# A planned order of attention and ReGLU feed-forward work, planned anew with other transfer times, one load hold moved, and the last copies split over two PSUM banks

## The chip, the cores and the metric

The kernel runs on one core of one Trainium2 chip. The metric is the device time of one execution in microseconds (us). A profiled execution also gives a span, from its first to its last instruction, which is about 2 us shorter than the device time.

## The reference, cut to what matters

There are 8 batches, 8 heads, 576 queries and 64 channels per head; 16 beacon keys and values stand in front of the 576 ordinary ones, so that each query sees up to 592 keys. The attention output of all batches (4608 tokens of 512 channels) goes through a feed-forward block with a ReLU gate. Inputs and output are float32.

```python
k_all = concatenate([beacon_k, k], axis=2); v_all = concatenate([beacon_v, v], axis=2)
scores = matmul(q, k_all.T) / sqrt(D);  scores = where(causal, -1e9, scores)
a = exp(scores - scores.max(-1)); a /= a.sum(-1) + 1e-09
x = (a @ v_all).transpose(0, 2, 1, 3).reshape(B * S, H * D)
out = (maximum(x @ w_gate, 0) * (x @ w_val)) @ w_out        # 512 -> 1536 -> 512
```

## The kernel before

**Work.** A batch is loaded through 8 staging tiles (`st`, 128x512 float32): K and Q by head pairs and "rests" (L545 to L628), V in 5 blocks (L631). Every staged tile is cast to bfloat16 (`rounded`, L511; V at L464 or L462), on POOL for all batches but the first, where DVE may do it as well (`ENG`). Q and K are then turned on TensorE (L522) and copied out of PSUM. Scores are computed in 64x64 tiles of the array (L740), one block of 64 queries against the keys that it may see. For each piece DVE adds the mask and takes the minimum (L688), ACT takes exp with the row sum (L695), DVE the reciprocal (L701), and POOL multiplies it in (L706). In the first batch TensorE turns the probabilities (L816); in the later ones a transposing DMA on SP's queue does (L826), one for each of four head pairs. The product with V (L836, in 128x64 tiles, and L859 for the last 16 queries) gives the token columns `xT`.

The feed-forward block takes the tokens in ten spans: 240, 336, seven times 512, and 448. I number them 0 to 9. A span is 12 times a gate (L897, relu on ACT at L908) and a value (L902, product on DVE at L913), four matmuls each, and then an output product (L928) of 12 matmuls for each 128 tokens, whose result is copied (L460 on ACT, L462 on DVE) and stored (L942). Spans 0 and 1 need the first batch alone; span 2 also needs the second.

**Weights.** They come by nine DMAs that POOL issues (L474): gate and value columns 0 to 511, 512 to 1023 and 1024 to 1535, then three row blocks of `w_out`. POOL runs in order, so each stands between other POOL work.

**The order.** No loop sets the order: every piece of work is a task with engines, a cost in us, dependences and a priority, and `Plan.order` (L183) lists them with a model of time: it takes the task that can begin first and, among those, the one of the lowest priority. A task that moves data also occupies a single "wire" for `move` us and ends a fixed time after that; a transfer may be begun at most `backlog` us before the wire is free (L203). Engines and queues then run in exactly the listed order, with semaphores. Costs and the constants at the head of the file (L20 to L57) so decide the order, and nothing else on the chip. `RANK1` is the priority of the second batch's loads.

Where the plan foresees an idle TensorE before its 160th us it lists fillers (L241 to L248): matmuls at L987 whose result nobody reads.

**Holds.** `HELD` (L38) ties three staging tiles of the second batch to weights: a one-element memset on POOL (L532) is planned after the named weight DMA has been issued, writes into the staging tile, and the tile's load waits for that write. Tile 0 is the K rest, tiles 2 and 4 are the K loads of its first two head pairs; SP's queue runs in order, so the loads behind them wait too.

**The end.** The last 64 tokens' output product is made in two halves of 256 columns, in two column tiles (partitions 0 to 63 and 64 to 127) of one bank. DVE copies one half, ACT the other, and SP and ACT each issue a store.

Of the kernel before, what the change touches and what calls it, by code (L numbers as in the profile page):

```python
# [16 lines left out]
BIG = 1e9  # L17


BACKLOG = 4.0  # L20
RANK1 = -19.0
AHEAD = 2.0
WWORK = -15.0
FILLED = 160.0
# [4 lines left out]
SWITCH = 0.1  # L29
# [5 lines left out]
PEQ = lambda b, g: b < 1  # L35
ENG = [("POOL", "DVE"), ("POOL",), ("POOL",)]
F_MOST = 3
HELD = {(1, 0): ("v", 0, 0), (1, 2): ("g", 0, 1024), (1, 4): ("v", 0, 1024)}  # L38
BEHIND = {(2, 7): (1, 1)}
MARK = 0.08  # L40
AB_FIRST = 0
# [8 lines left out]
W0 = 9.0  # L50
W_STEP = 3.4
W_ISSUE = 0.85
N_ST = 8
N_OSB = 3
FIRST_SPANS = [240, 336]
# [111 lines left out]
class Plan:  # L167
# [15 lines left out]
    def order(self):  # L183
        free = {}
        queue = {}
        for t in self.tasks:
            for e in t.engines:
                free.setdefault(e, 0.0)
                queue.setdefault(e, [])
        for t in self.tasks:  # L190
            if t.left == 0:
                for e in t.engines:
                    queue[e].append(t)
        wire = 0.0
        part = 0
        free["DMA"] = 0.8
        done = []

        def begin(t, e):
            at = t.ready  # L200
            if e == "DMA" or t.move:
                at = max(at, wire - self.backlog)
            for h in t.holds:  # L203
                if h.tile is None:
                    if h.prev is not None:
                        continue
                    if h.next is not None:
                        first = h.slots.first_pairs(sum(x.next is not None for x in t.holds))
                        if first is None:
                            return None  # L210
                        at = max(at, first)
                        continue
                    first = h.slots.first(sum(x.tile is None and x.slots is h.slots for x in t.holds) - 1)
                    if first is None:
                        return None
                    at = max(at, first)
            return max(at, free[e]), at

        while True:
            best = None  # L220
            for e in queue:
                for t in queue[e]:
                    times = begin(t, e)
                    if times is None:
                        continue
                    at, could = times
                    late = 0
                    if e == "PE":
                        late = -1 if part and t.part == part else 1 if part != t.part and at < t.ready + t.lazy else 0
                    key = (at, late, t.prio)  # L230
                    if best is None or key < best[0]:
                        best = (key, t, e)
            if best is None:
                break
            (at, _, _), t, e = best
            for x in t.engines:
                queue[x].remove(t)
            for h in t.holds:
                if h.tile is None:
                    if h.next is not None:  # L240
                        h.tile, h.next.tile = h.slots.take_pair()  # L241
                    else:
                        h.tile = h.slots.take()
            if e == "PE" and FILL_FROM < at < self.filled:
                since, tile = max(free[e], FILL_FROM), self.filler
                if at >= FILL_BANK:
                    first = min(self.banks.free, key=lambda f: f[:2], default=(at, 0, None))
                    since, tile = max(since, first[0]), first[2]  # L248
                n = int((at - since) * FILL / (0.11 if at > FILL_COLD else 0.22))
                if n > 0 and tile is not None:  # L250
                    done.append(Filler(n, tile, self.fill))
            t.start, t.engine = at, e
            cost = t.cost
            if e == "DMA":
                issue, move = cost
                if issue > 1.2:
                    wire = max(wire, at + 0.3) + move
                    free[e] = max(at + issue, wire - 0.2)
                else:
                    free[e] = at + issue  # L260
                    wire = max(wire, at + issue) + move
                end = max(wire, free[e]) + 1.9
            else:
                if isinstance(cost, dict):
                    cost = cost[e]
                if e == "PE":
                    cost += SWITCH * (t.part != part)
                    part = t.part
                free[e] = end = at + cost
                if t.move:  # L270
                    wire = max(wire, end) + t.move
                    end = wire + 1.9
            for h in t.holds:
                h.users -= 1
                if h.users == 0:
                    h.slots.give(end + (0.1 if e == "DMA" else LAGS[e] if t.lag is None else t.lag), h.tile)
            done.append(t)
            for u, then in [(u, end) for u in t.users] + [(u, free[e]) for u in t.soon]:
                u.ready = max(u.ready, then + (LAGS[e] if t.lag is None else t.lag))
                u.left -= 1  # L280
                if u.left == 0:
                    for x in u.engines:
                        queue[x].append(u)
        assert all(t.start is not None for t in self.tasks)
        self.end = max(free.values())
        return done
# [3 lines left out]
def kernel(  # L290
# [12 lines left out]
    nc = tc.nc  # L303
# [5 lines left out]
    P = 128  # L309
# [86 lines left out]
    def c_pe(n):  # L396
        return 0.003 + n / 2400.0
# [74 lines left out]
    def weight(kind, ko, kos, n0, w, prio, work):  # L472
        d, s = {"g": (wg_r, wg_s), "v": (wv_r, wv_s), "o": (wo_r, wo_s)}[kind]
        x = add("POOL", W_ISSUE, lambda t: nc.gpsimd.dma_start(  # L474
            d[:, ko:ko + kos, n0:n0 + w], s[:, ko:ko + kos, n0:n0 + w]), (), (), work, 0.1, move=0.78 * kos * w / 512,
            after=W0 + W_STEP * len(weight_in) / KM)
        for i in range(kos):
            for c in range(n0, n0 + w, 512):
                weight_in[kind, ko + i, c] = x
# [10 lines left out]
    def new_batch(b, prio, work):  # L490
# [140 lines left out]
        def load_v(c, prio):  # L631
            st = staged()
            rows = min(P, SK - P * c)

            def fetch(_):
                s3 = st.tile.rearrange("p (h d) -> p h d", h=H)
                if c == 0:
                    nc.sync.dma_start(s3[:Nb], heads(beacon_v, b, 0, Nb))
                    nc.sync.dma_start(s3[Nb:], heads(v, b, 0, P - Nb))
                else:  # L640
                    nc.sync.dma_start(s3[:rows], heads(v, b, P * c - Nb, rows))

            ld = add("DMA", (1.1 if c == 0 else 0.55, 1.54 * rows / P), fetch, (held,), (st,), prio[0])
            t.rows["v", c] = add(eng, cost, lambda x: copy(x.engine, t.v.tile[:rows, c, :], st.tile[:rows]),
                                 (ld,), (st, t.v), prio[1])

# [242 lines left out]
    def ffn(m0, mt, deps, prio):  # L889
# [26 lines left out]
        for t0 in range(0, mt, P):  # L916
# [1 line left out]

            halves = 2 if rows <= 64 else 1
            w = DM // halves  # L920
            ps, osb = Hold(f_s, 4 if halves == 1 else 3), [Hold(osb_s, 2) for _ in range(halves)]
            prev = prev if halves > 1 else None
            k = NF // 3 * (2 * halves - 1)
            for part in range(NF // k):
                def outp(_, part=part, t0=t0, rows=rows, ps=ps, w=w, halves=halves, k=k):
                    for nf in range(k * part, k * part + k):
                        for c in range(halves):
                            nc.tensor.matmul(ps.tile[64 * c:64 * c + rows, :w], hT[nf].tile[:, t0:t0 + rows],  # L928
                                             wo_r[:, nf, w * c:w * c + w], start=(nf == 0), stop=(nf == NF - 1))

                need = [prev] + hid[k * part:k * part + k] + [weight_in["o", nf, 0] for nf in range(k * part, k * part + k)]
                if part == 0:
                    need += hid[:11]
                prev = add("PE", k * c_pe(w) + SWITCH * (halves - 1), outp, need, (ps,) + tuple(hT[k * part:k * part + k]),
                           prio + 0.3 + 0.01 * part - (0.5 if part else 0))
            for c in range(halves):
                def evict(x, c=c, ps=ps, osb=osb[c], rows=rows, w=w):
                    copy(x.engine, osb.tile[64 * c:64 * c + rows, :w], ps.tile[64 * c:64 * c + rows, :w])

                def store(_, c=c, osb=osb[c], rows=rows, t0=t0, w=w):  # L940
                    q_ = nc.scalar if c else nc.sync
                    q_.dma_start(out[m0 + t0:m0 + t0 + rows, w * c:w * c + w], osb.tile[64 * c:64 * c + rows, :w])  # L942

                ev = add("ACT" if c else ("ACT", "DVE"), {"ACT": c_act(w), "DVE": c_dve(w)}, evict, (prev,), (ps, osb[c]), -1000 + prio)
                add("DMA", (0.4, 0.78 / halves), store, (ev,), (osb[c],), prio + OUT)


# [73 lines left out]
```

## Time and profile before

| | us |
|---|---|
| device time, median of 3 runs (405.5 to 406.61) | 406.01 |
| the profiled execution: device time | 406.85 |
| the profiled execution: span | 404.8 |
| PE busy | 390.3 |
| DVE busy | 293.9 |
| ACT busy | 260.1 |
| POOL busy | 234.7 |
| first gate matmul of span 0 | 25.45 |
| first gate matmul of span 2 | 94.70 |

Times inside the execution count from the start of its span. PE is TensorE, SP the engine whose queue issues most transfers. The busy time of PE is not its work: ends of matmuls are modelled, and a wait shorter than the pipeline hides in it. So the prediction goes by starts.

### The profile page before, as it was taken

How to read it: one execution, taken by the hardware profiler on the slowest of the kernel's cores; microseconds unless marked ns; L12 is line 12 of the kernel's file. 1: busy time of each engine (PE TensorE's matmuls, PEld its weight loads, DVE VectorE, ACT ScalarE, POOL GpSimd, SP SyncE). 2: the span in 40 equal slices, each digit the busy share in tenths (PEclk: the TensorE clock that was granted, in tenths of full speed). 3: DMA queues.
4: the chain of work that ended last, by engine and by line, in shares of the span. 5: the costliest groups of instructions: out<-in, count | busy, mean ns of one | idle time of the engine just before them, and what ended most of it. 6: DMA issues, size and time to landing. Idle time of an engine off the chain costs nothing.

```text
span 404.8 us, 9950 instructions
## 1 busy us (share of the span) xinstructions
PE 390.3 (96%) x3276; PEld 206.8 (51%) x3320; DVE 293.9 (73%) x1051; ACT 260.1 (64%) x809; POOL 234.7 (58%) x452
## 2 busy tenths in 40 slices
PE   7999999999999999999999899999999999999995
PEld 4667854655444545544455445454444454444542
DVE  3899798986977997769888977698777733442432
ACT  2989689768786786777776777588757721330320
POOL 6799779947395977567785768577565420000000
PEclk9999999999999999999999999999999999999999
DMA  7999997999999999959999999699948273001102
GB/s 179 215 193 216 240 223 147 185 206 204 203 202 217 236 187 275 185 161 189 254 181 201 228 230 177 171 255 226 172 78 175 42 147 123 0 0 53 52 2 91
DMA packets 174147, 67.99 MB, mean 168 GB/s; under 512 B 146384, under 2 KB 169552, under 8 KB 174096
## 3 DMA queue, kind: packets, MB, share of 16 engines
q1 hardware_dynamic: 169264, 62.57, 73.6%
q0 software_dynamic: 4752, 4.72, 7.6%
q8 instruction: 26, 0.43, 0.4%
q14 instruction: 25, 0.20, 0.2%
q10 hardware_dynamic: 80, 0.07, 0.1%
HBM read 38.54 MB, written 9.44 MB: 119 GB/s over the span
## 4 chain that ended last, share of the span: by engine, by line
PE 85%; DMA 5%; POOL 4%; DVE 2%; issue 2%; ACT 1%; SPq 1%; POOLq 0%; ACTq 0%; DVEq 0%
PE f L928 23%; PE f L902 22%; PE f L897 21%; PE f L740 6%; PE f L836 6%; PE f L522 4%; DMA wo_r<-in_moe_w_out_dram 2%; POOL xT L706 2%; DMA st<-in_v_dram 2%; PE f L816 1%; POOL pb L706 1%; PE f L987 1%; DMA st<-in_beacon_k_dram 1%; PE f L859 1%; PE f L790 1%
## 5 line engine op out<-in xcount | busy, mean ns | idle before, releaser
L706 POOL TENSOR_SCALAR pb<-pb,small 128x320 bf16<-128x320 bf16 (+8 forms) x272 | 142.1, 540 | 78.4 <-DVE small L701 73.5
L695 ACT ACTIVATE pb<-f,small 128x320 bf16<-128x320 f32 (+8 forms) x272 | 144.2, 553 | 22.7 <-DVE small L688 13.7
L688 DVE CUSTOM_DVE_ANT_0 f<-f,mask 128x320 f32<-128x320 f32 (+8 forms) x288 | 134.3, 517 | 12.1 <-PE f L740 7.2
L902 PE MATMUL f<-xT,wv_r 128*128 128x512 bf16 (+3 forms) x470 | 106.1, 358 | 0.5
L908 ACT ACTIVATE g<-f 128x512 f32<-128x512 f32 (+3 forms) x120 | 66.7, 565 | 60.6 <-PE f L897 53.8
L897 PE MATMUL f<-xT,wg_r 128*128 128x512 bf16 (+3 forms) x463 | 104.7, 357 | 0.9
L913 DVE TENSOR_TENSOR hT<-g,f 128x512 bf16<-128x512 f32 (+3 forms) x120 | 75.2, 632 | 38.1 <-PE f L902 34.7
L928 PE MATMUL f<-wo_r,hT 128*128 128x512 bf16 (+2 forms) x439 | 99.1, 374 | 1.9 <-issue 1.0
L897 PEld LDWEIGHTS <-wg_r 128*128 128x128 bf16 x480 | 45.3, 98 | 43.1 <-issue 1.2
L928 PEld LDWEIGHTS <-hT 128*128 128x128 bf16 (+2 forms) x456 | 41.9, 100 | 48.1 <-issue 4.0
L902 PEld LDWEIGHTS <-wv_r 128*128 128x128 bf16 x480 | 44.2, 98 | 42.3 <-issue 2.3
L695 ACT ACTIVATION_READ_ACCUMULATOR pb<-f,small 128x1 f32 x272 | 60.5, 222 | 0.0
L511 POOL TENSOR_SCALAR h<-st 128x512 bf16<-128x512 f32 (+1 forms) x92 | 48.6, 543 | 7.6 <-DMA st<-in_k_dram 3.1
L688 DVE DVE_READ_ACCUMULATOR2_ANT small<- 128x1 f32 x296 | 42.4, 143 | 0.2 <-issue 0.2
L740 PE MATMUL f<-kT,qT 64*64 64x64 bf16 (+7 forms) x640 | 35.9, 295 | 1.5 <-ACT pb L695 1.0
L462 DVE COPY osb<-f 128x512 f32<-128x512 f32 (+2 forms) x26 | 17.7, 681 | 24.0 <-PE f L928 24.0
L701 DVE RECIPROCAL small<-small 128x2 f32<-128x2 f32 (+3 forms) x144 | 22.1, 163 | 14.1 <-ACT pb L695 9.3
L522 PE MATMUL f<-ident,h 128*128 128x128 bf16 (+1 forms) x320 | 27.9, 219 | 2.5 <-POOL h L511 1.4
L522 PEld LDWEIGHTS <-h 128*128 128x128 bf16 (+1 forms) x320 | 21.0, 99 | 15.6 <-POOL h L511 5.8
L740 PEld LDWEIGHTS <-qT 64*64 64x64 bf16 x640 | 15.1, 106 | 23.9 <-issue 18.5
L836 PE MATMUL f<-pTb,v 128*64 128x320 bf16 (+3 forms) x488 | 26.0, 253 | 0.0
L836 PEld LDWEIGHTS <-v 128*64 128x64 bf16 (+1 forms) x512 | 20.6, 109 | 9.7 <-issue 7.2
(60 smaller groups left out, 236.0 us busy)
## 6 DMA issues: line engine op xcount, KB each, us to landing
out_dram<-osb SPq DMA_DIRECT2D x34, 256.0 KB, 2.2
st<-in_k_dram SPq DMA_DIRECT2D x32, 256.0 KB, 4.6
st<-in_q_dram SPq DMA_DIRECT2D x32, 256.0 KB, 5.1
st<-in_v_dram SPq DMA_DIRECT2D x24, 256.0 KB, 5.8
st<-in_v_dram SPq DMA_DIRECT2D x8, 224.0 KB, 6.3
wg_r<-in_moe_w_gate_dram POOLq DMA_DIRECT2D x3, 512.0 KB, 6.2
wv_r<-in_moe_w_val_dram POOLq DMA_DIRECT2D x3, 512.0 KB, 6.6
wo_r<-in_moe_w_out_dram POOLq DMA_DIRECT2D x3, 512.0 KB, 7.7
```

Of the source, the lines that this page charges most:

```text
L511: (nc.gpsimd if x.engine == "POOL" else nc.vector).tensor_scalar(to, src, by, 1.0, ALU.mult, ALU.mult)
L522: nc.tensor.matmul(to, h16.tile[:rows, a * P:(a + 1) * P], ident[:rows, :rows], start=True, stop=True)
L688: nc.vector.tensor_tensor_reduce(out=view(i, n - m), in0=view(i, n - m), in1=msk, scale=1.0, scalar=at(7) if m < n else 3.0e38, op0=ALU.ad ...
L695: nc.scalar.activation(ph.tile.rearrange("p a n -> p (a n)")[:, a:a + n], view(i), AF.Exp, bias=at(i), scale=-1.0, accum_out=at(4 + i))
L706: nc.gpsimd.tensor_scalar(one, one, at(8 + i), 1.0, ALU.mult, ALU.mult)
L740: nc.tensor.matmul(banks[k][b_].tile[64 * i:64 * i + 64, off:off + n], t.q.tile[r, 2 * g + i, 64 * j:64 * j + 64], t.kT.tile[r, 2 * g + i, ...
L836: nc.tensor.matmul(ps.tile[64 * hh:64 * hh + 64, d0:d0 + w], t.v.tile[:rows, c, D * h:D * h + D], rhs(64 * hh), start=(c == 0), stop=(c == ...
L897: nc.tensor.matmul(psg.tile[:, :mt], wg_r[:, ki, nf * P:(nf + 1) * P], xT[:, ki, m0:m0 + mt], start=(ki == 0), stop=(ki == KM - 1))
L902: nc.tensor.matmul(psv.tile[:, :mt], wv_r[:, ki, nf * P:(nf + 1) * P], xT[:, ki, m0:m0 + mt], start=(ki == 0), stop=(ki == KM - 1))
L908: r = add("ACT", c_act(mt), lambda _, psg=psg, g=g: nc.scalar.activation(g.tile[:, :mt], psg.tile[:, :mt], AF.Relu), (a,), (psg, g), -1000 ...
L913: hid.append(add("DVE", c_dve(mt), lambda _, psv=psv, g=g, nf=nf: nc.vector.tensor_mul(hT[nf].tile[:, :mt], g.tile[:, :mt], psv.tile[:, :m ...
L928: nc.tensor.matmul(ps.tile[64 * c:64 * c + rows, :w], hT[nf].tile[:, t0:t0 + rows], wo_r[:, nf, w * c:w * c + w], start=(nf == 0), stop=(n ...
```

## The change

Six constants of the plan change, one hold moves, and the last output product uses two banks instead of one.

- `BACKLOG` 4 to 6 us, `RANK1` -19 to -14.
- A weight block of 4 x 512 columns is planned to occupy the wire for 2.8 us instead of 3.12 (`W_MOVE` 0.7 for 0.78); a V block of 128 rows for 1.25 us instead of 1.54 (`V_MOVE`); every transfer is planned to end 1.8 us after the wire instead of 1.9 (`LAND`).
- The load of K for the second batch's first head pair is held behind the second value block (columns 512 to 1023) instead of the third gate block. The hold of the second head pair, behind the third value block, stays.
- In the last output product each half takes its own bank, with two users (product and copy) instead of three.

```diff
-BACKLOG = 4.0
-RANK1 = -19.0
+BACKLOG = 6.0
+RANK1 = -14.0
...
-HELD = {(1, 0): ("v", 0, 0), (1, 2): ("g", 0, 1024), (1, 4): ("v", 0, 1024)}
+HELD = {(1, 0): ("v", 0, 0), (1, 2): ("v", 0, 512), (1, 4): ("v", 0, 1024)}
...
+W_MOVE = 0.7
+V_MOVE = 1.25
+LAND = 1.8
...
-                end = max(wire, free[e]) + 1.9
+                end = max(wire, free[e]) + LAND
...
-                    end = wire + 1.9
+                    end = wire + LAND
...
-            d[:, ko:ko + kos, n0:n0 + w], s[:, ko:ko + kos, n0:n0 + w]), (), (), work, 0.1, move=0.78 * kos * w / 512,
+            d[:, ko:ko + kos, n0:n0 + w], s[:, ko:ko + kos, n0:n0 + w]), (), (), work, 0.1, move=W_MOVE * kos * w / 512,
...
-            ld = add("DMA", (1.1 if c == 0 else 0.55, 1.54 * rows / P), fetch, (held,), (st,), prio[0])
+            ld = add("DMA", (1.1 if c == 0 else 0.55, V_MOVE * rows / P), fetch, (held,), (st,), prio[0])
...
-            ps, osb = Hold(f_s, 4 if halves == 1 else 3), [Hold(osb_s, 2) for _ in range(halves)]
+            ps, osb = [Hold(f_s, 4 if halves == 1 else 2) for _ in range(halves)], [Hold(osb_s, 2) for _ in range(halves)]
...
-                            nc.tensor.matmul(ps.tile[64 * c:64 * c + rows, :w], hT[nf].tile[:, t0:t0 + rows],
+                            nc.tensor.matmul(ps[c].tile[64 * c:64 * c + rows, :w], hT[nf].tile[:, t0:t0 + rows],
...
-                def evict(x, c=c, ps=ps, osb=osb[c], rows=rows, w=w):
+                def evict(x, c=c, ps=ps[c], osb=osb[c], rows=rows, w=w):
```

Because the plan decides the order, the small edits reorder nearly the whole program. The instructions that do the kernel's work are the same on every engine but for who does a few casts and copies; fillers go from 103 to 98.

More of the change, by code (lines that the diff above doesn't have):

```diff
@@ L933, in ffn @@
                     need += hid[:11]
-                prev = add("PE", k * c_pe(w) + SWITCH * (halves - 1), outp, need, (ps,) + tuple(hT[k * part:k * part + k]),
+                prev = add("PE", k * c_pe(w) + SWITCH * (halves - 1), outp, need, tuple(ps) + tuple(hT[k * part:k * part + k]),
                            prio + 0.3 + 0.01 * part - (0.5 if part else 0))
             for c in range(halves):
-                def evict(x, c=c, ps=ps, osb=osb[c], rows=rows, w=w):
+                def evict(x, c=c, ps=ps[c], osb=osb[c], rows=rows, w=w):
                     copy(x.engine, osb.tile[64 * c:64 * c + rows, :w], ps.tile[64 * c:64 * c + rows, :w])
@@ L942, in store @@
                     q_.dma_start(out[m0 + t0:m0 + t0 + rows, w * c:w * c + w], osb.tile[64 * c:64 * c + rows, :w])
-                ev = add("ACT" if c else ("ACT", "DVE"), {"ACT": c_act(w), "DVE": c_dve(w)}, evict, (prev,), (ps, osb[c]), -1000 + prio)
+                ev = add("ACT" if c else ("ACT", "DVE"), {"ACT": c_act(w), "DVE": c_dve(w)}, evict, (prev,), (ps[c], osb[c]), -1000 + prio)
                 add("DMA", (0.4, 0.78 / halves), store, (ev,), (osb[c],), prio + OUT)
```

## Prediction

> **What bounds the kernel now.** I read the page first, then a table of stretches, the waits of TensorE, and the timelines of the places that these name. The page (busy tenths in 40 slices of 10.1 us):
>
> ```profile
> PE 390.3 (96%) x3276; PEld 206.8 (51%) x3320; DVE 293.9 (73%) x1051; ACT 260.1 (64%) x809; POOL 234.7 (58%) x452
> ...
> PE   7999999999999999999999899999999999999995
> ...
> PEclk9999999999999999999999999999999999999999
> DMA  7999997999999999959999999699948273001102
> ```
>
> TensorE is the bound, at full granted clock throughout, and the DMA engines are nearly full for 300 us. Only an order that wastes less of TensorE's time can help. The waste lies early, as the table by stretches shows (length, busy us and count by engine, clock, DMA share, GB/s; cut at the first gate matmul of span 0, the first scores of the second batch, the first DMA transpose, span 2, and the end of attention):
>
> ```profile
> 0.00:25.45 25.45, 21.57 (x224) 13.32 (x225) 17.68 (x107) 16.39 (x57) 19.51 (x47) 1.00 0.97 200
> 25.45:49.03 23.58, 23.32 (x308) 19.25 (x305) 20.73 (x79) 19.65 (x55) 21.68 (x39) 1.00 1.12 215
> 49.03:70.04 21.01, 19.45 (x168) 10.92 (x169) 19.63 (x89) 18.60 (x70) 17.09 (x34) 1.00 0.99 192
> 70.04:94.70 24.66, 24.49 (x257) 14.31 (x258) 21.91 (x83) 17.64 (x59) 17.70 (x36) 1.00 1.05 197
> 94.70:330.00 235.30, 231.22 (x1954) 114.96 (x1988) 188.51 (x658) 173.02 (x546) 158.74 (x300) 1.00 0.93 191
> 330.00:404.80 74.80, 70.25 (x376) 34.00 (x379) 25.45 (x40) 14.79 (x27) 0.00 (x0) 1.00 0.19 55
> ```
>
> From 25.45 to 94.70 TensorE is idle for 0.26 + 1.56 + 0.17 = 2.0 us and runs 27 of the 103 fillers, which at their median start spacing of 0.109 us are 2.9 us more. After 94.70 there are no fillers, and only two idle stretches of note, 1.03 us at 220 to 230 and 0.51 at 270 to 280. TensorE's waits in all:
>
> ```profile
> PE f L522 <- POOL h L511: 1.4, 2, 1.0
> PE f L740 <- ACT pb L695: 1.0, 2, 0.8
> PE f L522 <- ACT pb L695: 1.0, 1, 1.0
> ...
> PE f L928 <- DMA wo_r<-in_moe_w_out_dram: 0.3, 1, 0.3
> ```
>
> The second is at 57.8 and 61.2 (the second batch's scores wait until ACT has read a bank), the last at 66.6, where span 0's output product waits for the third block of `w_out`, which POOL issued only at 57.53. The third is at 227.2.
>
> **The change part by part.** The orders of both built programs give what is moved; the durations are of the trace.
>
> *TensorE's own work.* Every matmul of before is in the new order, except five fillers: 5 x 0.109 = -0.55 us. But changes between the full array and the small tiles of L740, L790 and L836 go from 187 to 200, 85 of them before span 2 instead of 74. What one costs shows where a score step stands among gate matmuls (start, us, what):
>
> ```profile
> 112.63 0.59 PE L897 MATMUL f<-xT,wg_r 128*128 128x512 bf16 x2
> 113.15 0.55 PE L740 MATMUL f<-kT,qT 64*64 64x512 bf16 x6
> ```
>
> The first score starts 0.52 us after the first of two gate matmuls. Two starts that follow each other in one shape are 0.215 us apart; the second one took 0.309, so a change costs 0.094 us. 13 more make **+1.22**: +1.03 before span 2 and +0.19 behind it. The Trainium skill (TensorEngine Tiling (Array Packing), Key Properties) says that changing the tiling mode drains the engine, which speaks against this change, and the trace agrees with it, by those 0.094 us; a reading of the order without the drain would come out 1.2 us lower.
>
> *POOL up to the first span.* In the new order the first gate weights are issued before the first V casts, at some 9 us instead of 16.5 (POOL, below), and POOL instead of DVE casts the third pair of K and Q loads. Their casts stood on DVE at 13.54 and 14.31, so POOL's first normalization (L706) moves from 13.73 to about 14.3 + 0.6 = 14.9.
>
> ```profile
> 13.73 2.85 POOL L706 TENSOR_SCALAR xT<-xT,small 128x64 bf16<-128x64 bf16 x6 [0.97 <-DVE small L701]
> 16.52 0.94 POOL L474 DMA_DIRECT2D wg_r<-in_moe_w_gate_dram  x1
> ...
> 53.16 0.94 POOL L706 TENSOR_SCALAR pb<-pb,small 128x64 bf16<-128x64 bf16 x2 [3.84 <-PE f L740]
> ...
> 57.53 0.79 POOL L474 DMA_DIRECT2D wo_r<-in_moe_w_out_dram  x1
> ```
>
> Between it and the 16th there now stand four weight issues (0.84 each with their gap), one cast of Q and two of V (0.6 each): 7.3 + 3.4 + 1.8 = 12.5 us, to 27.4 instead of 23.4. So span 0 begins some 4 us later, near 29.5. That is not lost whole: in the new order TensorE does 1.7 us more work and 14 more fillers (1.5 us) before span 0, and 13 + 6 fewer fillers behind it.
>
> *POOL from there to the second batch's scores.* Behind 23.4 POOL needed 23.6 us until the casts of K and Q of the first two pairs were done at 47.0. The new order has in this place 21 normalizations (13.0 us by their widths), four weight issues (3.2), and 4.7 of casts: 20.9, to 48.3. The first scores move from 49.03 to some 50.3.
>
> *The second batch's softmax.* All three `w_out` issues are now ahead of it, at some 31, 33 and 43 us. From POOL's first normalization of this batch (53.16, after 3.84 us idle) to the 22nd, which completes the second head pair at 70.0, POOL is never idle. Of these 16.8 us two `w_out` issues, 1.65, go, and three casts, 1.8, come partly into the idle time before. So the pairs are ready at 66 to 67 and near 70. Before, the first was ready near 65.5 by the same count, but its transpose, on SP's queue behind a store of span 0 that was issued at 69.59, since the product came late with `w_out`, started at 70.04. It can now start near 67, land 8 us later as before, and let the first values start at about 75.5, not 78.7. Counted from the orders with the trace's spacings, TensorE has 51.5 us of work and 91 fillers up to there, where it had 52.7 and 101: the 3.2 us that the values are earlier are 2.3 of less work and 0.9 of fewer waits. I take **-1.6** for waits up to span 2, the visible 1.56 of the third stretch; the ends are 0 and -3.7, namely the 2.0 of idle time from 25.45 on and some 1.7 by which matmuls there start later than their spacing allows while the row still counts as busy.
>
> *Holds and loads.* With one weight block fewer ahead, the first pair's hold is written near 23 us instead of 32.2, the second's at 29 instead of 35.3. Before, only 0.23 us of POOL's time went to waiting for a load there, so earlier loads gain nothing by themselves. Behind a held load SP's queue has only loads of the same batch, and nobody waits for those so early. At the second batch five load DMAs now stand between the second and third transpose (2.4 us of issue); the third and fourth landed 2.9 and 2.6 us before use, so this is covered, and costs a wait only beyond that.
>
> *Later batches.* Both later stalls are loads that land after the plan's time: POOL waited 1.27 us for a K load at 226.55 and 1.27 for a V load at 270.86, and TensorE behind it. The deeper backlog lets such loads be issued earlier, while the shorter V time makes the plan expect them earlier. No row decides between them. The ends are -1.54 and +5 (below); I take **-0.8**, one half of what is there.
>
> *The last copies.* The end before:
>
> ```profile
> 400.55 0.42 DVE L462 COPY osb<-f 64x256 f32<-64x256 f32 x1 [0.74 <-PE f L928]
> 401.00 0.37 ACT L460 COPY osb<-f 64x256 f32<-64x256 f32 x1 [9.87 <-DVE osb L462]
> 401.40 0.56 ACTq L942 DMA_DIRECT2D out_dram<-osb  x1
> ```
>
> ACT starts only when DVE is done. With two banks it waits for TensorE alone and starts near 400.6: **-0.4**, all of it at the end of the chain. The ends are 0 and -0.45, for SP's own store was issued at 401.0.
>
> **Sum.** Up to span 2: -0.55 + 1.03 - 1.6 = -1.1, so span 2 begins near 93.6. Behind it: +0.2 - 0.8 - 0.4 = -1.0. Together -2.1: a span of 402.7 where 404.8 was, a device time of 404.75 for that execution (406.85), which lies 0.84 over the median of 406.01. So the median becomes **403.9**.
>
> **Rivals.** (a) *The order now fits and TensorE never starves after 25 us.* For: the new order holds only 8 fillers behind span 0's start. Against: DVE is busy for 0.88 and 0.93 of the two stretches from 25.45 to 70.04, so that softmax can hardly come sooner. Then -3.7 up to span 2 instead of -1.6, and both late stalls go: 403.9 - 2.1 - 0.75 = 401.0. (b) *The early weights crowd out the last loads of the first batch, and nothing is won.* The DMA share is already 1.08 from 10 to 20 us, and a weight block was in flight for 6.2 us. Sharing half and half, the loads behind it come up to 3.1 us later, POOL's chain with them; then span 0's 4 us are 6 to 7, no wait goes, and the late stalls stay: 406.0 - 0.55 + 1.22 - 0.4 = 406.3. The Trainium skill (DMA: Bandwidth & Descriptors, Queues, rings and completion order) has each engine take turns between the queues with work, packet by packet; no row here tests it at 9 us. (c) *Slower: loads land late in every later batch.* The plan now counts a V block at 0.55 + 1.25 + 1.8 = 3.6 us when the wire is free, while its median from issue to landing is 5.8. If a late load stops POOL's casts, and TensorE behind them, by the 1.03 us of the stretch at 220 in four of the six later batches, it is 4 x 1.03 - 1.54 = +2.6 on top of (b) without its crowding: 408.9; in all six 411. It decides from the point where a cast starts over 1 us later than the turn behind it stands on TensorE. Against: TensorE waited so twice in six batches though the plan's V time was then longer. (d) *It does not do what it says.* The holds and the banks are in the built program; only the times could be no truer, which is (b).
>
> **Chances.** Forecast 0.46 (402.5 to 405.2), (a) 0.14, (b) with (d) 0.20, (c) 0.20. To leave out no more than 2 in 10 the range goes from 401.0 to 407.8. Differences under 0.3% (1.2 us) can hardly be measured here. Faster than 404.8: most of the forecast and (a), 0.57; within: 0.23; slower than 407.2: 0.20.
>
> **What would show it.** Right: span 2's first gate matmul near 93.6, no wait for `w_out`, a first DMA transpose near 67, 200 changes of tile, and the last two copies side by side. Wrong, if span 0 starts after 31, if TensorE idles before the second batch's first values, or if POOL's waits for K or V loads grow behind 100 us.

## The result and the profile after

| | before | after |
|---|---|---|
| device time, median of 14 runs each, us | 406.03 (404.56 to 408.08) | 409.08 (407.38 to 410.62) |
| ratio after to before, 95% interval | | 1.0067 [1.0048, 1.0085] |
| the profiled execution: device time, us | 406.85 | 408.42 |
| the profiled execution: span, us | 404.8 | 406.7 |

The changed kernel is slower by 0.67%, some 2.7 us by the ratio and 3.05 between the medians. The forecast was 403.9, faster by 2.1, and its range ended at 407.8.

The page of after, the rows that answer to those of before:

```profile
PE 391.3 (96%) x3272; PEld 205.6 (51%) x3315; DVE 294.9 (72%) x1052; ACT 259.3 (64%) x805; POOL 235.8 (58%) x455
...
PE   6699999999999999999999999999999999999995
...
PEclk9899999999999999999999999999999999999999
DMA  7999979998999799979999969994814682001102
```

TensorE's first two slices, up to 20 us, have become 6 and 6 (7 and 9 before), and the granted clock has an 8 in the second. The rest of the row is full: the stall in mid-order is gone, an early one has come. The table by stretches (columns as in the prediction) shows it; first before, then after:

```profile
10.00:20.00 10.00, 9.66 (x113) 6.43 (x111) 8.89 (x51) 9.74 (x40) 7.42 (x14) 1.00 1.08 215
20.00:30.00 10.00, 9.41 (x107) 6.26 (x106) 9.18 (x39) 8.68 (x31) 9.91 (x20) 1.00 1.19 192
```

```profile
10.00:20.00 10.00, 6.86 (x68) 4.38 (x67) 7.38 (x41) 5.24 (x28) 5.50 (x13) 0.89 1.15 237
20.00:30.00 10.00, 9.77 (x104) 5.83 (x103) 9.56 (x43) 8.87 (x28) 9.88 (x21) 0.94 1.24 216
...
50.00:70.00 20.00, 19.95 (x189) 12.18 (x186) 18.61 (x78) 17.11 (x59) 15.48 (x30) 1.00 0.79 192
```

From 10 to 20 us four engines do less than before and the DMA engines more. From 50 to 70 TensorE is now idle for 0.05 us, as was meant. TensorE's waits in after (what waited, for what: us in total, times, longest):

```profile
PE f L525 <- ACT xT L698: 2.1, 1, 2.1
...
PE f L525 <- POOL h L514: 1.8, 3, 1.0
PE f L525 <- DVE h L514: 1.1, 2, 0.7
```

L525 turns K and Q (L522 before). All three waits lie ahead of 19 us. The first names ACT, yet TensorE had been idle for 2.13 us up to 16.98, and POOL, at the same time, waited for a load. POOL's timeline of after:

```profile
8.67 0.94 POOL L477 DMA_DIRECT2D wg_r<-in_moe_w_gate_dram  x1
...
13.22 0.62 POOL L514 TENSOR_SCALAR h<-st 128x512 bf16<-128x512 f32 x1 [0.57 <-DMA st<-in_k_dram]
16.30 0.62 POOL L514 TENSOR_SCALAR h<-st 128x512 bf16<-128x512 f32 x1 [2.46 <-DMA st<-in_q_dram]
16.90 0.67 POOL L709 TENSOR_SCALAR xT<-xT,small 128x64 bf16<-128x64 bf16 x2
```

The first gate block is issued at 8.67 (before: 16.52). The Q load issued behind it, at 9.03, comes late, POOL waits 2.46 us for it, and the first normalization starts at 16.90, where 13.73 was and 14.9 was forecast. The transfers in flight just behind 9 us (KB, us from issue to landing), first before, then after:

```profile
st<-in_q_dram SPq DMA_DIRECT2D x1, 256.0 KB, 5.0
```

```profile
wg_r<-in_moe_w_gate_dram POOLq DMA_DIRECT2D x1, 512.0 KB, 7.1
...
st<-in_q_dram SPq DMA_DIRECT2D x1, 256.0 KB, 7.1
```

So the third Q load lands at 16.13 instead of 13.85; the K and Q loads of the fourth pair land at 17.47 and 18.41 instead of 14.74 and 15.81. What the two queues moved from 9 to 16 us (q1 has SP's loads, q0 POOL's weight blocks: packets, MB, share of the 16 engines), first before, then after:

```profile
q1 hardware_dynamic: 4997, 1.78, 124.1%
```

```profile
q1 hardware_dynamic: 3089, 1.20, 72.0%
q0 software_dynamic: 528, 0.52, 45.9%
```

Both together move 1.72 MB in after, 1.78 in before: the gate block's 0.52 MB do not come on top, SP's loads get 0.58 less. The end of after:

```profile
402.19 0.42 DVE L465 COPY osb<-f 64x256 f32<-64x256 f32 x1 [0.74 <-PE f L931]
402.23 0.37 ACT L463 COPY osb<-f 64x256 f32<-64x256 f32 x1 [9.44 <-PE f L931]
402.62 0.57 ACTq L945 DMA_DIRECT2D out_dram<-osb  x1
```

The two copies now run side by side.

For all kernels below I use three marks of the trace: the first weight load of a gate in span 0, in span 2 (0.24 us ahead of the matmul that the prediction names), and the last weight load of all. They are of one execution of each kernel.

| us | span 0 | span 2 | last |
|---|---|---|---|
| before | 25.45 | 94.46 | 400.13 |
| after | 32.30 | 95.94 | 401.78 |
| forecast, by the prediction's sum | 29.5 | 93.4 | 398.4 |

### The profile page after: what moved, and what is told of

It reads as the page before. It is cut to its first block, busy times and chain, and to the rows that moved or that the text cites. A ratio compares the mean times of both kernels' runs of the same rounds, so it can differ in the third digit from the quotient of the medians.

```text
span 406.7 us, 9970 instructions
## 1 busy us (share of the span) xinstructions
PE 391.3 (96%) x3272; PEld 205.6 (51%) x3315; DVE 294.9 (72%) x1052; ACT 259.3 (64%) x805; POOL 235.8 (58%) x455
## 4 chain that ended last, share of the span: by engine, by line
PE 86%; DMA 6%; issue 2%; DVE 2%; SPq 1%; POOL 1%; ACT 1%; DVEq 0%; POOLq 0%
PE f L931 23%; PE f L900 21%; PE f L905 21%; PE f L743 7%; PE f L839 6%; PE f L525 4%; DMA st<-in_k_dram 3%; DMA pTb<-pb 2%; PE f L990 2%; PE f L819 1%; DMA st<-in_q_dram 1%; PE f L862 1%; DVE f L691 1%; POOL h L514 1%; SPq L607 1%
## 5 line engine op out<-in xcount | busy, mean ns | idle before, releaser
L691 DVE CUSTOM_DVE_ANT_0 f<-f,mask 128x576 f32<-128x576 f32 (+8 forms) x288 | 134.2, 514 | 14.7 <-PE f L743 9.8
L931 PE MATMUL f<-wo_r,hT 128*128 128x512 bf16 (+3 forms) x438 | 99.1, 374 | 1.2 <-issue 0.6
L514 POOL TENSOR_SCALAR h<-st 128x512 bf16<-128x512 f32 (+1 forms) x94 | 50.2, 546 | 16.2 <-DMA st<-in_q_dram 4.8
L698 ACT ACTIVATION_READ_ACCUMULATOR pb<-f,small 128x1 f32 x272 | 59.2, 218 | 0.0
L465 DVE COPY osb<-f 128x512 f32<-128x512 f32 (+1 forms) x27 | 18.4, 681 | 25.4 <-PE f L931 24.2
L743 PE MATMUL f<-kT,qT 64*64 64x512 bf16 (+7 forms) x640 | 36.0, 295 | 0.3
L525 PE MATMUL f<-ident,h 128*128 128x128 bf16 (+1 forms) x320 | 29.3, 220 | 5.5 <-ACT xT L698 2.1
L704 DVE RECIPROCAL small<-small 128x1 f32<-128x1 f32 (+3 forms) x144 | 21.1, 160 | 14.2 <-ACT pb L698 9.6
L525 PEld LDWEIGHTS <-h 128*128 128x128 bf16 (+1 forms) x320 | 21.1, 99 | 20.2 <-POOL h L514 8.6
L467 POOL TENSOR_SCALAR v<-st 128x512 bf16<-128x512 f32 (+1 forms) x39 | 23.8, 620 | 4.7 <-DMA st<-in_v_dram 3.4
```

The lines of the kernel that those rows point to most:

```text
L514: (nc.gpsimd if x.engine == "POOL" else nc.vector).tensor_scalar(to, src, by, 1.0, ALU.mult, ALU.mult)
L525: nc.tensor.matmul(to, h16.tile[:rows, a * P:(a + 1) * P], ident[:rows, :rows], start=True, stop=True)
L691: nc.vector.tensor_tensor_reduce(out=view(i, n - m), in0=view(i, n - m), in1=msk, scale=1.0, scalar=at(7) if m < n else 3.0e38, op0=ALU.ad ...
L698: nc.scalar.activation(ph.tile.rearrange("p a n -> p (a n)")[:, a:a + n], view(i), AF.Exp, bias=at(i), scale=-1.0, accum_out=at(4 + i))
L743: nc.tensor.matmul(banks[k][b_].tile[64 * i:64 * i + 64, off:off + n], t.q.tile[r, 2 * g + i, 64 * j:64 * j + 64], t.kT.tile[r, 2 * g + i, ...
L931: nc.tensor.matmul(ps[c].tile[64 * c:64 * c + rows, :w], hT[nf].tile[:, t0:t0 + rows], wo_r[:, nf, w * c:w * c + w], start=(nf == 0), stop ...
```

## The experiments

Theory A: the early gate block shares the DMA engines with the last K and Q loads of the first batch, and this alone makes the loss. Rivals: the loss lies in the later order (tile changes, loads of later batches), or it comes from the clock that TensorE loses when it idles. Each run is compared with runs of the kernel before on the same chip; these had medians of 404.84 (e1 to e4), 405.03 (e5 to e8) and 406.23 (e9 to e12), so ratios are used across them. The expectations of e1 to e6 reckon with 406.0 for the kernel before and 409.1 for the changed one, so their times are to be read as differences from these.

**e1, the gate block late in the new order.** `place` finds a task in the planned list by its name.

```diff
-    for t in plan.order():
+    done = plan.order()
+    x = done.pop(place(("g", 0, 0)))
+    done.insert(place(("v", 0, 0)), x)
+    for t in done:
         t.run(t)
```

> The changed kernel with one instruction moved: POOL issues the first gate weight block directly ahead of the first value block (near 15 us) instead of at 8.7; every other queue keeps its order. Theory A (the early block crowds the last loads of the first batch, TensorE runs dry and its clock is halved for a while): the third Q load lands before 14.5 us instead of 16.1, TensorE's wait of 2.1 us near 15 us goes, the clock stays at 1.00 in every stretch, and the median falls by 2 to 3 us, to 406 to 407. Theory B (the casts on POOL and the new order itself cost the time: tile changes and later stalls): the wait shrinks at most by half, and the median stays within 0.7 us of 409.1.

Measured: 404.75, ratio 0.9981 [0.9958, 1.0004]. One instruction, moved, takes 0.86% away again, 3.5 us, a little more than the 2 to 3 that were expected. The load behind 9 us and the stretch, in this kernel:

```profile
st<-in_q_dram SPq DMA_DIRECT2D x1, 256.0 KB, 4.9
```

```profile
10.00:20.00 10.00, 8.14 (x87) 5.03 (x84) 9.10 (x49) 7.84 (x38) 7.93 (x16) 1.00 1.08 214
```

The Q load is back to 4.9 us, the clock to 1.00; from 9 to 16 us SP's queue moves 1.77 MB again. Marks: 29.40, 92.90, 398.00. This is the prediction's own picture: 29.5 for span 0 and 93.4 for span 2 had been forecast, for an order whose loads land as before.

**e2, the gate block early in the order of before.**

```diff
+    x = done.pop(place(("g", 0, 0)))
+    done.insert(place(("cast", 0, "k", 1, 0)) + 1, x)
```

> The kernel before with the same instruction moved the other way: POOL issues the first gate block right behind its cast of the first batch's second K pair (near 9 us) instead of at 16.5. Theory A: the four loads behind it land 2 to 3 us later, TensorE gets waits near 15 us that the kernel before has not, perhaps with half clock, and the median rises by 2 to 3 us to 408 to 409. Theory B: 406.0, within 0.7 us, since the order is still that of before.

Measured: 407.99, ratio 1.0076 [1.0048, 1.0105]: the same loss, 3.1 us, without anything else of the change. TensorE's waits, the stretch, and the K load of the fourth pair (before 4.8 us) with the block beside it:

```profile
PE f L523 <- DVE h L512: 2.2, 1, 2.2
PE f L523 <- POOL h L512: 2.2, 3, 1.0
```

```profile
10.00:20.00 10.00, 6.96 (x71) 4.65 (x72) 5.90 (x33) 6.91 (x31) 4.92 (x11) 0.90 1.05 220
```

```profile
wg_r<-in_moe_w_gate_dram POOLq DMA_DIRECT2D x1, 512.0 KB, 8.5
...
st<-in_k_dram SPq DMA_DIRECT2D x1, 256.0 KB, 8.0
```

Here the block is in flight from 8.8 to 17.3, the third Q load (issued 8.9, landed 13.3) is on time, and the fourth pair is late (17.7 and 19.3). Which of the loads are hit so differs from the changed kernel; why is open. Marks: 27.98, 96.69, 401.19. Theory A stands: the later order isn't needed for the loss. No run moves the block with fewer bytes, so that its bytes do it, and not the act of issuing, rests on what the queues moved.

**e3, two banks alone.** Of the change only the last product's hunks, on the kernel before.

> The kernel before with the last output product in two banks, and nothing else. By the prediction ACT's copy starts with DVE's and the end comes 0.4 us sooner: 405.6. The rival: SP's store, which is issued when it always was, now ends last, so that 0.2 us or less is won: 405.8 to 406.0.

Measured: 404.53, ratio 0.9981 [0.9957, 1.0006]: not resolved. Its profile settles more. From the first of the last copies to the last landing it has 398.23 to 400.97, 2.74 us, like after (402.19 to 404.93), where before had 400.55 to 403.44, 2.89. So the two banks win 0.15 us and not 0.4: the copies overlap, but SP's store, which before was issued first and landed first, is now issued just behind ACT's (402.64 in after, 398.68 in e3), lands 2.29 us later in both instead of 2.00, and is the last.

And this kernel has the whole order of before, but not its late stalls. PE's part of the stretches, first before, then e3:

```profile
220.00:230.00 10.00, 8.97 (x119) 1.00 1.07 214
...
270.00:280.00 10.00, 9.49 (x77) 1.00 1.17 197
```

```profile
220.00:230.00 10.00, 9.90 (x114) 1.00 1.09 265
...
270.00:280.00 10.00, 9.89 (x66) 1.00 1.06 219
```

The stalls of 1.03 and 0.51 us belonged to one execution, not to the order; e2 and e12, which keep this order too, have 9.95 at 220. TensorE's early wait for a `w_out` block does belong to this order, but its size changes from execution to execution: 0.3 us in before, none in e2 and e3, 0.8 in e12, 1.4 in e11. Marks of e3: 25.08, 93.77, 397.82. It is the better baseline for what an order is worth.

**e4, filling the gap.** The changed kernel with 23 more fillers ahead of the two turns that TensorE waits to do.

```diff
+    done.insert(place(("turn", 0, "q", 0, 1)), Filler(19, fill_bank, fill))
+    done.insert(place(("turn", 0, "k", 0, 1)), Filler(4, fill_bank, fill))
```

> The changed kernel with 23 more fillers on TensorE, 4 ahead of the turn of the first batch's third K load and 19 ahead of that of the third Q load, where it waited 0.5 and 2.1 us; the loads stay as late as they are. If the halved clock is what costs (3.41 us at half speed, so up to 1.7 us a time): the clock stays at 1.00 until 30 us and the median falls by 1 to 1.7 us, to 407.4 to 408.1. If the late loads alone cost: the clock may stay up but the median stays within 0.5 us of 409.1.

Measured: 408.01, ratio 1.0073 [1.0047, 1.0098].

```profile
10.00:20.00 10.00, 8.71 (x96) 6.49 (x93) 6.87 (x36) 5.83 (x29) 5.68 (x13) 1.00 1.17 224
```

The clock stays at 1.00 and TensorE is 1.85 us busier than in after, but span 0 begins at 31.57 and span 2 at 95.20, and the ratio is that of after within the intervals. (408.01 as such lies in the range of the other case, but before took only 404.84 on this chip.) By the marks the halved clock is worth 0.7 us at most; it isn't the cause of the 3. The data are late.

**e5 and e6, which part of the change does it.** On the kernel before, the planned transfer times alone (e5, three constants) and the backlog alone (e6). In both built programs, and in neither with the rank or the hold alone, the planner puts the gate block early.

```diff
-                end = max(wire, free[e]) + 1.9
+                end = max(wire, free[e]) + 1.8
...
-        ... move=0.78 * kos * w / 512,
+        ... move=0.7 * kos * w / 512,
...
-        ... 1.54 * rows / P), ...
+        ... 1.25 * rows / P), ...
```

```diff
-BACKLOG = 4.0
+BACKLOG = 6.0
```

> The kernel before with one part of the change alone: the planned transfer times (2.8 us for 3.12 of a weight block, 1.25 for 1.54 of a V block, 1.8 for 1.9 behind the wire). In this order the first gate block again stands right behind the cast of the second K pair on POOL (row 20 of POOL instead of 29), and TensorE has 209 changes of tile for 187 and 131 fillers for 103. Theory A, the early gate block costs some 3 us wherever it stands there: 407.5 to 409, with the first gate block issued near 9 us and the third K and Q loads over 2 us late. Rival, the loss belongs to the holds and the rank of the second batch's loads, or to the whole order: 404 to 406.

> The kernel before with the other part that moves the first gate block in the plan: BACKLOG 6 for 4 alone, planned transfer times as before. POOL issues the first gate block in row 20 again; 202 changes of tile, 131 fillers. Theory A: 407.5 to 409, like the run with the transfer times alone, so that each of the two parts brings the loss on its own and the two together not twice. Rival, the deeper backlog lets all loads come earlier and pays for it: 404 to 406.

Measured: e5 416.91, ratio 1.0292 [1.0255, 1.0329]; e6 420.27, ratio 1.0377 [1.0337, 1.0418]. Both were missed, by both theories: each part alone costs 12 to 15 us, the whole change 3. In e5 the gate block is in flight from 8.6 to 18.2 and the fourth pair lands at 18.5 and 19.4:

```profile
PE f L522 <- DVE h L511: 3.2, 1, 3.2
```

```profile
10.00:20.00 10.00, 5.41 (x56) 3.41 (x53) 5.80 (x31) 5.24 (x28) 4.54 (x10) 0.92 1.03 218
20.00:30.00 10.00, 10.00 (x94) 5.73 (x94) 8.90 (x38) 6.30 (x21) 9.21 (x20) 0.74 1.03 167
```

Around 3.2 us of waiting the clock falls: TensorE runs at half of it from 18.4 to 25.2 us, and from 19.1 on with full work. How much of the 12 us is the block, e9 was to tell.

**e9, e5 with the gate block late.** The two lines of e1 on e5.

> The kernel before with the planned transfer times alone (416.91 us as the planner lists it), and the one POOL instruction of the first gate block taken from behind the second K pair's cast to directly ahead of the first value block. Nothing else moves; 209 changes of tile and 131 fillers stay. Theory A, the early block delays the last K and Q loads: those loads land 2.5 to 4 us earlier, the waits of TensorE for the casts (3.2 and 2.1 us) go, and so does the half clock that TensorE then had under full work from 18.4 to 25.2 us (up to 3.4 us): 409 to 412. What is left over the kernel before is then this order's own work, 22 changes at 0.094 and 28 fillers at 0.109: 5.1 us, 410.1. Rival, most of the 12 us is the order itself and the block has its 3 us only: 413.5 to 415.

Measured: 414.30, ratio 1.0196 [1.0165, 1.0226], 3.9 us less than e5 by the ratios. The block has its 3 to 4 us here as well, though in this pair the half clock under full work (6.8 us long, so up to 3.4) may hold much of it. Theory A's 409 to 412 is missed; the rival, that most of e5's loss is its own order, is right. What that order has more than before: 22 tile changes (2.4 us at the 0.11 of e11), 28 fillers (3.05 at 0.109; 30 stand between 140 and 160 us, where before has none), and 3.4 us at half clock from 72.0 on, behind a gap of 2.08 us (up to 1.7). These prices add up to 7.1 of the 8.0 us; that these are the causes was not tested, and e6 was not taken apart.

**e11 and e12, the price of a tile change.** One dead matmul of 64 columns ahead of each of the last 48 gates and values, overwritten by what follows: in a 64x64 tile (`Z = 64`, e11) or in the full array (`Z = 128`, e12).

```diff
+                if m0 >= M0:
+                    nc.tensor.matmul(psg.tile[:Z, :64], ident[:Z, :Z], mask.bitcast(BF16)[:Z, :64], start=True, stop=True)
                 for ki in range(KM):
                     nc.tensor.matmul(psg.tile[:, :mt], wg_r[:, ki, nf * P:(nf + 1) * P], xT[:, ki, m0:m0 + mt],
```

> The kernel before with 48 added matmuls whose result is overwritten, one ahead of each gate and each value of the last two spans, where no attention stands: 64x64 tile, 64 columns. To be compared with the next run, where the same 48 are in the full 128x128 array: the difference is 96 changes between the full array and the small tile. At the 0.094 us that the prediction read: 9.0 us more than the next run, some 416. Rival, such a change hides behind the weight loads or belonged to that one place: the two runs agree within 1 us.

> Control of the run before: the same 48 added matmuls in the full array. 48 matmuls of 64 columns, a filler of 256 columns takes 0.109: by columns 0.03 to 0.06 each, so 1.3 to 2.9 us over the kernel before: 406.3 to 408.2.

Measured: 418.30 and 407.09, 11.2 us for 96 changes, 0.117 each. Between the marks of span 8 and the last the profiles differ by 69.99 - 59.62 = 10.37 us, 0.108 each. One stretch of either timeline, first e11, then e12:

```profile
343.89 1.04 PE L908 MATMUL f<-xT,wv_r 128*128 128x512 bf16 x4
344.86 0.21 PE L906 MATMUL f<-mask,ident 64*64 64x64 bf16 x1
345.00 1.04 PE L908 MATMUL f<-xT,wv_r 128*128 128x512 bf16 x4
```

```profile
343.56 1.03 PE L908 MATMUL f<-xT,wv_r 128*128 128x512 bf16 x4
344.43 0.19 PE L899 MATMUL f<-mask,ident 128*128 128x64 bf16 x1
344.45 1.03 PE L901 MATMUL f<-xT,wg_r 128*128 128x512 bf16 x4
```

From group to group it is 1.11 us with two changes and 0.89 without: 0.11 for one. The rival, that the two runs agree within 1 us, is out. The prediction's 0.094 came from one place; 13 changes are 1.4 us.

**e7, e8 and e10, a better order.** On the changed kernel, `W0` is the time from which the planner may issue the first weight block.

```diff
-W0 = 9.0
+W0 = 14.0
```

e7 is this; e8 has `RANK1 = -19.0` as well; e10 has `W0 = 12.0` and the two lines of e1.

> The changed kernel with one constant: the planner may issue the first weight block from its 14th us instead of its 9th (W0), and the others as much later. The first gate block then stands in POOL's row 25 behind all the early casts of V, as in the run that moved this instruction by hand, with 194 changes of tile and 94 fillers for the 200 and 98 of the changed kernel. Theory A: the 3 us come back, and 6 changes at 0.094 and 4 fillers at 0.109 are 1.0 us less work than the run with the moved instruction (404.75): 403.5 to 404.8. Rival, the later blocks now come late for the spans or for the holds of the second batch: 406 or more, with TensorE waiting for a weight tile.

> The changed kernel with the first weight block planned from the 14th us on and the rank of the second batch's loads back at -19. 189 changes of tile and 95 fillers. If a change of tile costs what the prediction read (0.094 us) and fillers what they last, 5 fewer changes than with the 14 alone are 0.5 us: 403.0 to 404.5. If the lower rank of the loads was worth something by itself, this is slower than the 14 alone, by up to 1 us.

> The changed kernel with weights planned from the 12th us on (W0 12 for 9), and the first gate block moved by hand to directly ahead of the first value block, as in the first experiment. 193 changes of tile and 85 fillers, for 194 and 94 with the planner's own 14 (404.51). If fillers cost their 0.109 us wherever they stand, 403.4; if they stand in time that TensorE has to wait anyway, 404.5. Beating both kernels would need under 404.

| | us | ratio to before | span 0 | span 2 | last |
|---|---|---|---|---|---|
| e7 | 404.51 | 0.9988 [0.9972, 1.0004] | 27.66 | 93.70 | 397.57 |
| e8 | 405.97 | 1.0020 [1.0000, 1.0039] | 26.28 | 95.77 | 399.93 |
| e10 | 404.31 | 0.9940 [0.9918, 0.9962] | 25.77 | 91.39 | 398.46 |

e7 came as theory A has it: one constant for the planner is worth as much as the move by hand. The 1.0 us that it was to have over e1 isn't there (ratios 0.9988 and 0.9981, the same within the intervals). e8 was a miss: by the ratios 1.3 us slower than e7, more than either of its cases allowed. It has five tile changes fewer, but TensorE waits 1.5 us for the second value block up to 34.62, and is idle for 1.9 from 30 to 50. That this is why isn't shown: e10 waits 1.0 us for such a block up to 33.69, is idle for 1.5 in the same stretch, and is the fastest by ratio. e10 is the only kernel here whose interval lies below the kernel before, and beats after too; its expectation put that under 404, and it took 404.31 on a chip where before took 406.23. What it wins stands at span 2, at 91.39 where e11 and e12, with the order of before up to there and on the same chip, have 95.71 and 95.03; these two wait 1.4 and 0.8 us for `w_out`, e10 doesn't. The rest is open: its profiled span, 402.7, is no shorter than e7's 402.4 on another chip, so that the 9 fillers it saves against e7 aren't shown to be the cause.

## Why the prediction was wrong

**The step that failed: "POOL up to the first span".** It saw the gate block move to "some 9 us instead of 16.5" and priced POOL's order alone: one issue more ahead of POOL's normalizations, "that is not lost whole". The block's own bytes were left to rival (b). Measured: the loads behind it 2.3 to 2.7 us later, POOL's first normalization at 16.90 and not 14.9 (14.46 in e1), span 0 at 32.30 and not 29.5, behind the 31 that the prediction had named as a sign of being wrong, and all of the difference kept: +2.9 at span 0, +3.0 at span 2, +3.8 at the end (after against e1). In after TensorE has nothing behind 30 us to absorb it with: 20.00 busy of 20 from 30 to 50, 19.95 from 50 to 70. In the order of before the delay is kept too (e2 against e3: +2.9, +2.9, +3.4), though TensorE is idle for 1.5 us from 30 to 70 in both; that idle time moves along with the delay instead of taking it up. Three pairs that differ in this instruction alone show 3.5 us (after, e1), 3.1 (e2, before) and 3.9 (e5, e9).

**Rival (b) had the mechanism and the wrong price.** Its delay ("up to 3.1 us later") and its span 0 ("6 to 7" us late, measured 6.85) were right. But it turned that into "nothing is won", 406.3, at a chance of 0.20: it took the gains out and put no loss in. With TensorE full behind 30 us the delay itself had to be added: 406.3 + 2.9 = 409.2, and 409.08 was measured. So close a fit is partly luck: the 2.9 was read afterwards, and two other terms of the 406.3 were off by 0.2 each (below), in one direction. The Trainium skill (DMA: Bandwidth & Descriptors, Queues, rings and completion order) says that each engine takes turns between the queues that have work, packet by packet. The 0.52 MB that POOL's queue moved from 9 to 16 us while SP's moved 0.58 less agree, and so do the Q load's 7.1 us beside the block, 5.0 and 4.9 without it; but in e2 that load took 4.4 beside the block, and only those behind it 8.0 and more.

**Waits up to span 2, -1.6: right in the main, once the loads are on time.** From 30 to 70 us TensorE is idle for 0.07 us in e1, where e3 has 1.46, and the first transpose starts at 66.31 (e3 69.35; 67 had been forecast; 69.0 in after). The waits for ACT (1.0 us in e3) are gone, and neither after nor e1 waits for `w_out`, as the order of before does for 0 to 1.4 us. e1 reaches span 2 at 92.90, e3 at 93.77: -0.87, where -1.1 stood as the sum of all steps up to there. Single executions do not settle the size.

**Later batches, -0.8: wrong.** It was half of two stalls that e3 shows to be of one execution, not of the order. There was nothing to win. From span 2 to the last mark e1 needs 305.10 us, e3 304.05: the new order is 1.05 longer there, of which two tile changes more explain 0.2. (After and e4, of the same order as e1, need 305.84 and 305.95; e2, of e3's, 304.50.) The rest is open; the idle time behind 100 us is about the same (3.1 and 3.0).

**Tile changes, +1.22:** mis-sized a little, 1.4. **Last copies, -0.4:** 0.15, since SP's store took over the end; the prediction used that store for the bound of this term, but left it where it was.

**The time of reference.** The sum was made against the profiled execution's 406.85 and then lowered by 0.84 to the median. That execution held 1.5 us of late stalls, which the -0.8 then counted once more as something to be won. Without that term the forecast's steps come to -1.3, so 404.7; with the measured sizes of the tile changes and the last copies to -0.9, so 405.1. e1's ratio of 0.9981 makes 405.2 of the same 406.0. The interval reaches up to 1.0004, though, and e3, in the old order, has 0.9981 too: that the new order with its loads on time wins anything isn't shown.

**Rival (c)** did not occur: behind 100 us TensorE waits for POOL's casts once in after, for 0.3 us. That its 408.9 lies next to the measured 409.08 is luck. **(a)** came true from 30 to 70 us only.

## What to carry to other kernels

A transfer that is issued earlier is not free because its issue is: ask which loads are in flight with it, who waits for them, and whether the bound engine has any slack behind that place to take the delay up. If it has none, the delay goes into the end in full; idle time in which it waits for work that is delayed as well is no slack. And a stall in one profile is worth nothing until a second execution of the same order shows it again.

## What the runs showed of the hardware

TensorE's granted clock fell to one half for 3.4 us, or twice that, 1.7 to 3.7 us after the start of each idle gap of 2.08 us or more behind the first 10 us (after 2.13, e2 2.19, e9 2.08, e5 3.22, e6 3.31 and 3.15) and after none of up to 1.50 us (e8 1.50, e7 1.42, e11 1.39, e4 1.02). The Trainium skill (TensorE: Matmul & The Clock Gate, Part 1) gives an idle window of about 3.4 us for it; here gaps of two thirds of that were enough. In the changed kernel the fall cost nothing that the medians show (e4 against after: 1.0073 and 1.0067) and at most 0.7 us by the marks.
